# Batch 0's first tiles as seven block products, last value groups in 64 rows, and a new order up to pair 17

## The chip, the cores and the metric

The kernel runs on one core of one Trainium2 chip. The metric is the device time of one execution in microseconds. The five engines are named as the profile does: PE (matmuls; PEld is its weight loads), DVE, ACT, POOL and SP, which issues most DMAs.

## What is computed

Cosine attention over 8 batches of 12 heads, 448 positions and 64 columns a head, followed by a two-layer network with a hard-swish between:

```python
q_n = q / (np.linalg.norm(q, axis=-1, keepdims=True) + 1e-06)
k_n = k / (np.linalg.norm(k, axis=-1, keepdims=True) + 1e-06)
scores = np.matmul(q_n, k_n.transpose(0, 1, 3, 2)) / tau
attn = softmax(scores)
x = np.matmul(attn, v)                  # to (3584, 768)
h = x @ w_in                            # (768, 2048)
g = h * np.clip(h + 3.0, 0.0, 6.0) / 6.0
out = g @ w_out                         # (2048, 768)
```

## The kernel before

Heads are taken two at a time: 6 pairs a batch, 48 pairs in all. For each pair, the steps have two-letter names, which the written order uses. `LQ` and `LV` load q, k and v (DMAs on SP). `SQ` squares an item, on ACT, POOL or DVE as its letter says; `RE` sums the squares (DVE, L236); `NO` makes the reciprocal norms with four activations (ACT, L252 to L255); `NM` multiplies them in (mostly POOL, L267). An item j is one pair's-worth of q or k; its raw data lie in a ring of buffers in the large tile `big`. `TR` transposes on PE (up to item 13), `XD` by a transposing DMA on SP from item 14 on; `CQ`, `CK` and `CS` copy the result to where scores read it. `SC.i.g` are the scores of pair i, in four groups g: three of 2 x 128 keys and a last one, M, that holds the last 64 keys of both heads; they are matmuls over 64 rows (L415). `EX` takes their exponentials (ACT, L433). `VC` casts the values, `VA.i.g` multiplies exponentials by values into the PSUM tile PV (L455, 8 matmuls of 65 columns a group), and `FI` divides by the row sums (DVE, L475 and L476). `BK` with `CX`, or the DMAs `XP` and `XB`, bring the result into `xT`.

The network's work is a stream of units taken from by `U`. A first-layer unit (`mm1_unit`, L566) is 6 matmuls of 448 columns; `UA` is its clip on ACT (L575) and `UV` the product on DVE (L581), which writes `gT`. The second layer runs on output tiles of 128 tokens. Before the change, batch 0's tiles 0 to 2 are six units `mm2_unit` (3 tiles, two halves of the output columns, 16 matmuls of 384 columns each, L613). All other tiles are taken in pairs, as a 2 x 2 block product with seven products instead of eight: `product_unit` (L739, 8 matmuls each), named 1 to 7, with sums of g (`g_sum`, L717, DVE), sums of w_out's blocks (`weight_sums`, L688, DVE) and sums of results on POOL (`both`, `rest`, L768 to L772, and L780). The sums y3 and y4 are written over blocks of w_out, so they come after the last unit that reads those blocks, and after sums 1 and 6, or 1 and 7, which read them too.

Six PSUM banks serve as a ring for scores, transposes and units; a bank is taken again once its readers are done. Each engine runs its instructions in the order in which they are written. Up to pair 17 that order is `PLAN`, a list of steps written out by hand, with `ORDER` saying which units the stream holds; from pair 18 (`FIRST`) on it is a loop with fixed places, its units in `units` and its sums in `side`. In the plan the last value group reads all 128 rows, the other head's half of the value tile being zero; in the loop it reads 64:

```python
rows = slice(64 * h, 64 * h + 64) if name == "M" and i >= FIRST else slice(0, 128)
```

`D` and `DP` are matmuls on zeros that fill PE early on. `W` starts one of eight DMAs of weights on POOL's queue.

Of the kernel before, what the change touches and what calls it, by code (L numbers as in the profile page):

```python
# [10 lines left out]
AF = mybir.ActivationFunctionType  # L11
# [3 lines left out]
EPS = 1e-6  # L15


FIRST = 18
ORDER = "111111111111111111111111111111222222"

PLAN = [
# [36 lines left out]
]  # L58


# [1 line left out]
def kernel(  # L62
# [10 lines left out]
    nc = tc.nc  # L73
    B, H, S, D = q.shape
# [59 lines left out]

    def raw_before(j):

        return j - NR if j < 26 else j - NR + 2

    def raw_buffer(j):
        return raws[j % NR if j < 26 else (j - 26) % (NR - 2)]  # L140

    sqs = [item(NR + i) for i in range(2)]
    nrms = [const.tile([128, 7, 2, D], BF16, name=f"nrm{i}", tag=f"nrm{i}") for i in range(3)]
# [21 lines left out]
    def needs(*what):  # L165
        for w in what:
            assert w in issued or any(x < 0 for x in w[1:] if isinstance(x, int)), w
# [76 lines left out]
    def norms(d, *items):  # L244

        needs(("NM", 2 * d - 4), ("NM", 2 * d - 3))
        items = items or (0, 1)
        for x in items:
            needs(("RE", 2 * d + x))
        it = slice(items[0], items[-1] + 1)  # L250
        ln, nr, le, r = (t[:, it, :] for t in rs[d % 2])
        nc.scalar.activation(out=ln, in_=n2s[d % 2][:, it, :], func=AF.Ln)  # L252
        nc.scalar.activation(out=nr, in_=ln, func=AF.Exp, scale=0.5)
        nc.scalar.activation(out=le, in_=nr, func=AF.Ln, bias=EPS)
        nc.scalar.activation(out=r, in_=le, func=AF.Exp, scale=-1.0)  # L255
        for x in items:
            issued.add(("NO", d, x))

# [184 lines left out]
    def q_cols(b, j):  # L443
        return slice(128 * j, 128 * j + 128)

    def values(i, g):
        needs(("VC", i), ("FI", i - 1), *values_after(i, g))
        at = at_of.pop((i, g))
        vt = vx[i % NVX]
        last = g == (3 if i < FIRST else 2)  # L450
        for n, name in enumerate(GROUPS[g]):
            for j in range(4):
                for h in (range(2) if name == "M" else ["AB".index(name[0])]):
                    rows = slice(64 * h, 64 * h + 64) if name == "M" and i >= FIRST else slice(0, 128)
                    nc.tensor.matmul(  # L455
                        pv_out(j, h),
                        at[rows, n, q_cols(i // HP, j)],
                        vt[rows, 3 + h if name == "M" else 5 * h + int(name[1]), :],
                        start=(name in ("A0", "B0") and j == 0),
                        stop=last,  # L460
                        skip_group_check=True,
                    )
# [67 lines left out]
    def tail(c, n):  # L530

        assert 2 * RAW <= c and c + n <= (NR + 2) * RAW + NV * VAL
        return big[:, c : c + n]
# [102 lines left out]

    def second(b):
        assert b % 2 == 0
        return [(mm2_unit, b, t, m) for m in (1, 0) for t in range(3)]

# [1 line left out]


    LEFT, RIGHT = slice(0, MH), slice(MH, 2 * MH)
    PAIRS = [p for b in range(0, B, 2) for p in (((b, 0), (b, 1)), ((b + 1, 3), (b + 1, 0)), ((b + 1, 1), (b + 1, 2)))][1:]
    LOOP = 8
    summed, g_summed, issued_products = set(), set(), set()
    banks, parts, ready = {}, {}, set()  # L650
    late_sums = [
# [3 lines left out]
    late_sums[0].pop("e")  # L655
    TAIL += 7 * SUM
    wide = [big[:, c : c + MH] for c in range(0, 3 * MH, MH)]
    wide_late = [tail(c, MH) for c in range(TAIL, TAIL + 2 * (len(PAIRS) - LOOP) * MH, MH)]

    def sum_of(n, what):  # L660

        if what == "e":
            return gs["1"] if n < B - 2 else late_sums[1]["e"]
        if n < LOOP or n == len(PAIRS) - 1:
            return gs[what + str(n % 2) if what == "7" else what]
        return late_sums[n % 2][what]

# [2 lines left out]
            return wide[n % 2], wide[2]  # L670
        return wide_late[2 * (n - LOOP) : 2 * (n - LOOP) + 2]

    def weight_sums(what, c0, n):

        w = w_out_sb[:, :, :].rearrange("p (c k) m -> p c k m", k=2)[:, c0 : c0 + n]
        b11, b12, b21, b22 = (w[:, :, k, m] for k in range(2) for m in (LEFT, RIGHT))
# [8 lines left out]
        }[what]  # L685
        if what in w_sum:
            o = w_sum[what][:, c0 : c0 + n, :]
        nc.vector.tensor_tensor(out=o, in0=x, in1=y, op=op)  # L688
        summed.update((what, c) for c in range(c0, c0 + n))

    def half(b, t, k):
# [143 lines left out]
    def sums(n, names):  # L835
        return [(g_sum, n, x) for x in names]
# [4 lines left out]
    def products(text):  # L841
# [17 lines left out]
    }  # L859
    APART = {(n, y) for n in range(len(PAIRS)) for x, y in (("5a", "3"), ("2a", "4")) if f"{x}.{n}" in " ".join(TURNS.values()).split()}  # L860
    side = {
        18: [(weight_sums, "y4", KC // 2, KC // 2)], 19: sums(0, "62"), 20: sums(0, "1"),
        21: sums(1, "75"), 22: sums(1, "621"),
        25: sums(2, "75"), 26: sums(2, "62"), 27: sums(2, "1"), 28: [(g_left, 2)], 29: sums(2, "e"),
        31: sums(3, "75"), 32: sums(3, "62"), 33: sums(3, "1"),
# [70 lines left out]
    def finish_units(e):  # L936
        post[e].pop(0)()

    def whole_units(n, engines="av"):
# [4 lines left out]
                    finish_units(e)  # L944

    OPS = {
        "LQ": load_qk, "LV": load_v, "W": next_weights, "SQ": square, "RE": reduce, "NO": norms,
        "NM": normalise, "VC": vcast, "TR": transposes, "XD": crossbar, "XB": back_crossbar, "XP": back_two, "CQ": copy_q, "CK": copy_k, "CS": copy_k3, "SC": scores,
        "EX": exps, "VA": values, "FI": finish_values, "BK": back, "CX": copy_x, "U": unit, "UA": lambda: finish_units("a"), "UV": lambda: finish_units("v"),
        "GL": g_left, "WS": lambda x, *h: weight_sums(str(x), *((h[0] * KC // 2, KC // 2) if h else (0, KC))), "UU": whole_units, "D": busy, "DP": busy_pv, "OPEN": open_ring,  # L950
    }

    def do(op, *args):
        OPS[op](*args)
        key = (op,) + tuple(a for a in args if isinstance(a, int))
        if op not in ("RE", "NM", "LQ"):
            issued.add(key[:3] if op == "SC" else key)

    def run(text):
# [133 lines left out]
```

## Time and profile before

| | us |
|---|---|
| median of 3 runs (405.72 to 407.1) | 405.85 |
| the profiled execution's own time | 405.02 |
| its span, first to last instruction | 403.2 |
| PE busy | 394.5 |
| DVE busy | 286.4 |
| ACT busy | 266.2 |
| POOL busy | 233.2 |
| granted PE clock, mean | 1.00 of full |

The span starts with the first instruction and ends with the last; busy time is a union, and matmuls overlap, so that a busy PE can still hold gaps between starts. Stretches of the span are told in us from its start. The unchanged first steps of the plan end near 34 us, pair 18 begins near 113 us.

### The profile page before, as it was taken

The numbers are of one execution on the slowest core, as the hardware profiler recorded it, in microseconds if no ns is written. First come the engines' busy times: TensorE is split into PE (matmuls) and PEld (weight loads), VectorE is DVE, ScalarE is ACT, GpSimd is POOL, SyncE is SP. The second block draws the span as 40 slices with busy tenths as digits, with TensorE's granted clock in tenths as the row PEclk, the third lists the DMA queues.
The fourth block names the chain that finished last, engine by engine and source line by source line (L and its number), as shares of the span: only waits on it lengthen the run. The fifth ranks groups of instructions, "written<-read, shape, count | busy, mean of one in ns | idle before, by whom it ended". The sixth has DMA issues, their size and how long they took to land.

```text
span 403.2 us, 9617 instructions
## 1 busy us (share of the span) xinstructions
PE 394.5 (98%) x3696; PEld 233.7 (58%) x3696; DVE 286.4 (71%) x501; ACT 266.2 (66%) x609; POOL 233.2 (58%) x228
## 2 busy tenths in 40 slices
PE   7999999999989999999999999999999999999996
PEld 5666556555655556555555556555565556555564
DVE  6898768766998676776857878687656666644663
ACT  6899998787557686776758768668648755224230
POOL 7899664562294996489386875776665500510070
PEclk9999999999999999999999999999999999999999
DMA  8999989989989559885989659986864523130133
GB/s 290 308 241 276 200 249 239 144 126 221 193 204 231 120 119 228 176 224 130 181 214 210 134 143 171 183 193 145 191 150 82 112 46 67 40 79 20 27 73 99
DMA packets 91566, 65.32 MB, mean 162 GB/s; under 512 B 56064, under 2 KB 89984, under 8 KB 91520
## 3 DMA queue, kind: packets, MB, share of 16 engines
q1 hardware_dynamic: 87408, 58.02, 62.8%
q0 software_dynamic: 3712, 6.29, 9.1%
q8 instruction: 29, 0.48, 0.5%
q10 hardware_dynamic: 400, 0.39, 0.3%
q14 instruction: 17, 0.14, 0.1%
HBM read 47.19 MB, written 11.01 MB: 144 GB/s over the span
## 4 chain that ended last, share of the span: by engine, by line
PE 94%; DVE 3%; DMA 1%; POOL 1%; ACT 0%; issue 0%; SPq 0%; DVEq 0%
PE M L566 24%; PE M L739 17%; PE PV L455 13%; PE Y L566 6%; PE M L415 6%; PE Z L566 5%; PE Y L739 4%; PE Z L739 4%; PE M L613 3%; PE M L819 2%; PE Z L415 2%; PE PV L921 2%; PE Z L819 1%; PE Y L415 1%; PE SC L415 1%; DMA big<-in_q_dram 1%
## 5 line engine op out<-in xcount | busy, mean ns | idle before, releaser
L433 ACT ACTIVATE at<-M 128x448 bf16<-128x448 f32 x200 | 99.6, 565 | 17.7 <-PE M L415 15.5
L566 PE MATMUL M<-xT,w_in_sb 128*128 128x448 bf16 x522 | 110.7, 353 | 0.0
L566 PEld LDWEIGHTS <-w_in_sb 128*128 128x128 bf16 x768 | 71.9, 98 | 62.5 <-issue 2.6
L267 POOL TENSOR_TENSOR nrm<-big,r 128x896 bf16<-128x896 f32 (+1 forms) x48 | 79.4, 1658 | 26.7 <-ACT r L255 18.5
L581 DVE SCALAR_TENSOR_TENSOR gT<-u,M 128x448 bf16<-128x448 bf16 x76 | 46.8, 618 | 35.6 <-ACT u L575 35.3
L455 PEld LDWEIGHTS <-at 128*128 128x128 bf16 (+1 forms) x1536 | 54.8, 97 | 24.1 <-issue 14.8
L224 POOL TENSOR_TENSOR big<-big 128x896 f32<-128x896 f32 (+3 forms) x39 | 63.8, 1639 | 8.0 <-DMA big<-in_k_dram 4.1
L575 ACT ACTIVATE u<-M 128x448 bf16<-128x448 f32 x87 | 48.8, 561 | 29.5 <-PE M L566 29.1
L455 PE MATMUL PV<-vx,at 128*128 128x65 bf16 (+1 forms) x1536 | 64.3, 194 | 0.2 <-DVE on L476 0.2
L236 DVE TENSOR_REDUCE n<-big 128x14 f32<-128x896 f32 (+1 forms) x50 | 51.8, 1040 | 3.9 <-ACT big L222 3.4
L372 POOL COPY km<-tT 64x128 bf16<-64x128 bf16 x34 | 12.4, 364 | 59.3 <-DMA tT<-nrm 43.4
L768 POOL TENSOR_TENSOR big<-big 128x384 f32<-128x384 f32 x11 | 12.0, 1088 | 55.1 <-ACT big L787 55.0
L739 PEld LDWEIGHTS <-gT 128*128 128x128 bf16 x288 | 27.8, 98 | 20.2 <-DVE gT L717 0.6
L739 PE MATMUL M<-w_out_sb,gT 128*128 128x384 bf16 x208 | 37.9, 326 | 0.1
L433 ACT ACTIVATE at<-Z 128x448 bf16<-128x448 f32 x49 | 27.6, 564 | 10.4 <-PE M L415 8.8
L286 POOL CAST vx<-big 128x512 bf16<-128x512 f32 x44 | 33.0, 754 | 2.4 <-DMA big<-in_v_dram 2.4
L476 DVE TENSOR_TENSOR on<-PV,rc 128x512 bf16<-128x512 f32 x48 | 33.2, 691 | 1.7
L415 PE MATMUL M<-tT,kz 64*128 64x448 bf16 (+1 forms) x175 | 31.9, 351 | 1.0 <-DVE o L626 1.0
L739 PEld LDWEIGHTS <-gs 128*128 128x128 bf16 x224 | 21.6, 98 | 14.5
L566 PE MATMUL Y<-xT,w_in_sb 128*128 128x448 bf16 x132 | 28.6, 353 | 0.0
L433 ACT ACTIVATE at<-Y 128x448 bf16<-128x448 f32 x45 | 25.6, 568 | 3.3 <-PE Z L415 3.1
L739 PE MATMUL M<-w_sum,gs 128*128 128x384 bf16 x144 | 26.3, 326 | 0.0
(131 smaller groups left out, 553.9 us busy)
## 6 DMA issues: line engine op xcount, KB each, us to landing
big<-in_v_dram SPq DMA_DIRECT2D x96, 128.0 KB, 4.7
big<-in_k_dram SPq DMA_DIRECT2D x24, 448.0 KB, 4.9
big<-in_q_dram SPq DMA_DIRECT2D x24, 448.0 KB, 4.3
out_dram<-o SPq DMA_DIRECT2D x107, 96.0 KB, 2.2
w_in_sb<-in_moe_w_in_dram POOLq DMA_DIRECT2D x4, 768.0 KB, 9.1
w_out_sb<-in_moe_w_out_dram POOLq DMA_DIRECT2D x4, 768.0 KB, 9.7
tT<-nrm SPq DMA_TRANSPOSE x34, 3.4
xT<-on SPq DMA_TRANSPOSE x25, 3.8
```

Of the source, the lines that this page charges most:

```text
L224: engines[e].tensor_tensor(out=o, in0=i, in1=i, op=ALU.mult)
L236: nc.vector.tensor_reduce(out=n2s[d % 2][:, j % 2, c], in_=sq[:, :, :, :].rearrange("p g c d -> p (g c) d")[:, c, :], axis=AX.X, op=ALU.add,)
L267: engines[e].tensor_tensor(out=nrm[:, :, g, :].rearrange("p c g d -> p g c d"), in0=raw_of[j][:, g, :, :], in1=rs[d % 2][3][:, j % 2, :] . ...
L286: (engines[e].copy if e == "a" else engines[e].tensor_copy)(out=o, in_=f)
L415: nc.tensor.matmul(o, ks, qt[rows], start=True, stop=True)
L433: nc.scalar.activation(out=o, in_=x, func=AF.Exp, scale=inv_tau)
L455: nc.tensor.matmul(pv_out(j, h), at[rows, n, q_cols(i // HP, j)], vt[rows, 3 + h if name == "M" else 5 * h + int(name[1]), :], start=(name ...
L476: nc.vector.tensor_tensor(out=on[:, :, :, :].rearrange("p j h d -> p h j d"), in0=pv4[:, :, :, 0:D], in1=rc[:, :, :].to_broadcast([128, 2, ...
L566: nc.tensor.matmul(ps[:, 0:S], w_in_sb[:, cc, fc * 128 : (fc + 1) * 128], x[:, cc, 0:S], start=(cc == 0), stop=(cc == CC - 1),)
L575: nc.scalar.activation(out=u[:, :], in_=ps[:, 0:S], func=AF.Relu, bias=0.5, scale=1.0 / 6.0)
L581: nc.vector.scalar_tensor_tensor(out=g[:, fc, c0 : c0 + S], in0=u[:, :], scalar=1.0, in1=ps[:, 0:S], op0=ALU.min, op1=ALU.mult,)
L739: nc.tensor.matmul(m, lhs[:, c, :], rhs[:, c, c0 : c0 + width], start=(base is None and c == 0), stop=(c == KC - 1), skip_group_check=True,)
```

## The change

The steps of the plan up to the opening of the ring of PSUM banks (`OPEN`) stay. From there to pair 17's turn the order is a new one, with these differences in what is done:

- Batch 0's tiles 0 and 1 become a block product of number -1 (`FOREMOST`): seven products of 8 matmuls in place of four units of 16. Tile 2 keeps its two units of 16. The products' sums of g (`GS.-1.x`, five) and their result sums on POOL (`UP`, the operations of `both`, `rest` and two additions) are new; the products 5 and 2 stand apart from 3 and 4, in banks of their own.
- The sums of w_out are made in halves and earlier: eight halves on DVE, two (of sums 6 and 7) on POOL. The half of y4 that ran beside pair 18 goes into the plan.
- The last value groups of pairs 4 and 6 to 16 read 64 rows (`.h`).
- Norms 6 run as two activations (`NA`) and two DVE operations (`ND`).
- Three filler matmuls go. Some squares, casts and copies change engine: ACT takes three value casts and seven more copies, DVE four more casts.
- The raw items 19 to 25 use five buffers instead of seven (as items from 26 on did before), since the two others hold the new product's results.

```diff
-ORDER = "111111111111111111111111111111222222"
+ORDER = "111111111111111111111111111111222222222"
...
-    "BK.3.Y VA.4.1 LQ.12 CS.6.v OPEN DP.2 CX.3.v NO.5 SC.6.0 VA.4.2 VA.4.3 SC.6.1 SC.6.2 EX.6.0 NM.8.p FI.4 EX.6.1",
+    "BK.3.Y VA.4.1 LQ.12 CS.6.v OPEN NO.5 NM.8.p CX.3.a SC.6.0 VA.4.2 VA.4.3.h SC.6.1 SC.6.2 NM.9.p EX.6.0 FI.4",
...
-    "CK.17.v XD.18 U EX.16.1 SQ.20.a.0.7 NM.19.p FI.15 WS.6 U UV XD.19 SC.16.3 RE.20 GL.0 WS.1 WS.7.0 EX.16.2 U VA.16.0 UA VA.16.1 LV.11",
...
-    "XP.14 NO.10 FI.16 NM.20.p CK.18.v U CK.19.v WS.7.1 WS.y3 WS.y4.0 XB.16 EX.17.2 UV UA VA.17.0 VC.18.p EX.17.3 RE.22 CS.18.v",
...
+    "LQ.19 VA.12.3.h UA U RE.17 NO.8 GS.-1.6 GL.0 GS.-1.7 UA UV U FI.12 EX.13.2 NM.17.p U UV VC.15.v CK.14.v U",
+    "VA.13.0 UA UV SC.13.3 NM.16.p XD.17 U W U UA UA SQ.19.a.0.7 SQ.18.p.0.7 U CS.14.v WS.1.v.0 UV UV LV.9 RE.19",
+    "UA UA SC.14.0 WS.6.p.0 CK.15.v EX.13.3 U UV UA LV.8 VA.13.1 EX.14.0 RE.18 UA U VA.13.2 UV UA UV VC.14.a",
+    "VA.13.3.h SC.14.1 EX.14.1 UV SQ.20.a.0.7 UV SC.14.2 FI.13 U EX.14.2 LQ.22 UA U SC.14.3 WS.1.v.1 EX.14.3",
+    "WS.7.p.0 WS.6.v.1 GS.-1.2 UA NO.9 U WS.y3.v.0 WS.y3.v.1 LQ.21 WS.7.v.1 U UV VA.14.0 XD.16 UV WS.y4.v.0",
+    "SC.15.0 UA WS.y4.v.1 SC.15.1 EX.15.0 GS.-1.5 SC.15.2 VA.14.1 VC.17.a VA.14.2 NM.18.v U EX.15.1 SC.15.3 U",
...
-        return j - NR if j < 26 else j - NR + 2
+        return j - NR if j < 19 else j - NR + 2
...
+    def powers(d, *items):
...
+        nc.scalar.activation(out=ln, in_=n2s[d % 2][:, it, :], func=AF.Ln)
+        nc.scalar.activation(out=nr, in_=ln, func=AF.Exp, scale=0.5)
...
+    def reciprocals(d, *items):
...
+        nc.vector.tensor_scalar_add(out=le, in0=nr, scalar1=EPS)
+        nc.vector.reciprocal(out=r, in_=le)
...
-                    rows = slice(64 * h, 64 * h + 64) if name == "M" and i >= FIRST else slice(0, 128)
+                    apart = name == "M" and (i >= FIRST or halves)
+                    rows = slice(64 * h, 64 * h + 64) if apart else slice(0, 128)
...
-        return [(mm2_unit, b, t, m) for m in (1, 0) for t in range(3)]
+        return [(mm2_unit, b, 2, m) for m in (1, 0)] + products(f"3.{FOREMOST} 4.{FOREMOST} 5a.{FOREMOST} 2a.{FOREMOST} 1.{FOREMOST} 6.{FOREMOST} 7.{FOREMOST}")
...
-    def weight_sums(what, c0, n):
+    def weight_sums(what, c0, n, e="v"):
...
-        nc.vector.tensor_tensor(out=o, in0=x, in1=y, op=op)
+        engines[e].tensor_tensor(out=o, in0=x, in1=y, op=op)
...
-        18: [(weight_sums, "y4", KC // 2, KC // 2)], 19: sums(0, "62"), 20: sums(0, "1"),
+        19: sums(0, "62"), 20: sums(0, "1"),
```

More of the change, by code (lines that the diff above doesn't have):

```diff
@@ L135, in raw_before @@
     def raw_before(j):
-        return j - NR if j < 26 else j - NR + 2
+        return j - NR if j < 19 else j - NR + 2
     def raw_buffer(j):
-        return raws[j % NR if j < 26 else (j - 26) % (NR - 2)]
+        return raws[j % NR if j < 19 else (j - 19) % (NR - 2)]
     sqs = [item(NR + i) for i in range(2)]
@@ L255, in norms @@
         nc.scalar.activation(out=r, in_=le, func=AF.Exp, scale=-1.0)
+        for x in items:
+            issued.add(("NO", d, x))
+    def powers(d, *items):
+        needs(("NM", 2 * d - 4), ("NM", 2 * d - 3))
+        items = items or (0, 1)
+        for x in items:
+            needs(("RE", 2 * d + x))
+        it = slice(items[0], items[-1] + 1)
+        ln, nr = (t[:, it, :] for t in rs[d % 2][:2])
+        nc.scalar.activation(out=ln, in_=n2s[d % 2][:, it, :], func=AF.Ln)
+        nc.scalar.activation(out=nr, in_=ln, func=AF.Exp, scale=0.5)
+        for x in items:
+            issued.add(("NA", d, x))
+    def reciprocals(d, *items):
+        items = items or (0, 1)
+        for x in items:
+            needs(("NA", d, x))
+        it = slice(items[0], items[-1] + 1)
+        nr, le, r = (t[:, it, :] for t in rs[d % 2][1:])
+        nc.vector.tensor_scalar_add(out=le, in0=nr, scalar1=EPS)
+        nc.vector.reciprocal(out=r, in_=le)
         for x in items:
@@ L444, in q_cols, with values @@
         return slice(128 * j, 128 * j + 128)
-    def values(i, g):
+    def values(i, g, halves=""):
         needs(("VC", i), ("FI", i - 1), *values_after(i, g))
@@ L638, in second @@
         assert b % 2 == 0
-        return [(mm2_unit, b, t, m) for m in (1, 0) for t in range(3)]
+        return [(mm2_unit, b, 2, m) for m in (1, 0)] + products(f"3.{FOREMOST} 4.{FOREMOST} 5a.{FOREMOST} 2a.{FOREMOST} 1.{FOREMOST} 6.{FOREMOST} 7.{FOREMOST}")
     LEFT, RIGHT = slice(0, MH), slice(MH, 2 * MH)
-    PAIRS = [p for b in range(0, B, 2) for p in (((b, 0), (b, 1)), ((b + 1, 3), (b + 1, 0)), ((b + 1, 1), (b + 1, 2)))][1:]
-    LOOP = 8
+    PAIRS = [p for b in range(0, B, 2) for p in (((b, 0), (b, 1)), ((b + 1, 3), (b + 1, 0)), ((b + 1, 1), (b + 1, 2)))]
+    FOREMOST, LAST, LOOP = -1, len(PAIRS) - 2, 8
+    PAIRS = dict(enumerate(PAIRS, FOREMOST))
     summed, g_summed, issued_products = set(), set(), set()
@@ L657 @@
     wide = [big[:, c : c + MH] for c in range(0, 3 * MH, MH)]
-    wide_late = [tail(c, MH) for c in range(TAIL, TAIL + 2 * (len(PAIRS) - LOOP) * MH, MH)]
+    wide_late = [tail(c, MH) for c in range(TAIL, TAIL + 2 * (LAST + 1 - LOOP) * MH, MH)]
     def sum_of(n, what):
@@ L663, in sum_of @@
             return gs["1"] if n < B - 2 else late_sums[1]["e"]
-        if n < LOOP or n == len(PAIRS) - 1:
+        if n < LOOP or n == LAST:
             return gs[what + str(n % 2) if what == "7" else what]
@@ L859 @@
     }
-    APART = {(n, y) for n in range(len(PAIRS)) for x, y in (("5a", "3"), ("2a", "4")) if f"{x}.{n}" in " ".join(TURNS.values()).split()}
+    APART = {(n, y) for n in PAIRS for x, y in (("5a", "3"), ("2a", "4")) if n == FOREMOST or f"{x}.{n}" in " ".join(TURNS.values()).split()}
     side = {
-        18: [(weight_sums, "y4", KC // 2, KC // 2)], 19: sums(0, "62"), 20: sums(0, "1"),
+        19: sums(0, "62"), 20: sums(0, "1"),
         21: sums(1, "75"), 22: sums(1, "621"),
@@ L946 @@
     OPS = {
-        "LQ": load_qk, "LV": load_v, "W": next_weights, "SQ": square, "RE": reduce, "NO": norms,
+        "LQ": load_qk, "LV": load_v, "W": next_weights, "SQ": square, "RE": reduce, "NO": norms, "NA": powers, "ND": reciprocals,
         "NM": normalise, "VC": vcast, "TR": transposes, "XD": crossbar, "XB": back_crossbar, "XP": back_two, "CQ": copy_q, "CK": copy_k, "CS": copy_k3, "SC": scores,
-        "EX": exps, "VA": values, "FI": finish_values, "BK": back, "CX": copy_x, "U": unit, "UA": lambda: finish_units("a"), "UV": lambda: finish_units("v"),
-        "GL": g_left, "WS": lambda x, *h: weight_sums(str(x), *((h[0] * KC // 2, KC // 2) if h else (0, KC))), "UU": whole_units, "D": busy, "DP": busy_pv, "OPEN": open_ring,
+        "EX": exps, "VA": values, "FI": finish_values, "BK": back, "CX": copy_x, "U": unit, "UA": lambda: finish_units("a"), "UV": lambda: finish_units("v"), "UP": lambda: finish_units("p"),
+        "GL": g_left, "GS": lambda n, what: g_sum(n, str(what)), "WS": lambda x, e, *h: weight_sums(str(x), *((h[0] * KC // 2, KC // 2) if h else (0, KC)), e), "UU": whole_units, "D": busy, "DP": busy_pv, "OPEN": open_ring,
     }
@@ L955, in do @@
         key = (op,) + tuple(a for a in args if isinstance(a, int))
-        if op not in ("RE", "NM", "LQ"):
+        if op not in ("RE", "NM", "LQ", "NA", "ND"):
             issued.add(key[:3] if op == "SC" else key)
```

39 rows, old and new, of the table PLAN are left out of this document.

## The prediction

> **What bounds the kernel now.** I read the page's engine totals first, then busy time by stretch, then the chain that ended last, then the groups and the timeline for prices.
>
> ```profile
> span 403.2 us, 9617 instructions
> PE 394.5 (98%) x3696; PEld 233.7 (58%) x3696; DVE 286.4 (71%) x501; ACT 266.2 (66%) x609; POOL 233.2 (58%) x228
> ```
> ```profile
> 34.40:67.00 32.60, 32.60 (x411) 20.22 (x409) 24.29 (x59) 29.95 (x72) 19.14 (x19) 1.00 1.02 235
> 67.00:90.00 23.00, 23.00 (x219) 12.36 (x217) 16.90 (x31) 18.40 (x43) 16.40 (x16) 1.00 0.92 152
> 90.00:112.60 22.60, 22.60 (x205) 13.56 (x204) 18.85 (x27) 15.26 (x37) 7.08 (x7) 1.00 1.03 207
> 112.60:120.00 7.40, 6.39 (x64) 3.60 (x63) 7.08 (x7) 3.74 (x9) 7.26 (x7) 1.00 0.87 217
> ```
>
> The rows of the second view are stretches: their length, then busy time of PE, weight loads, DVE, ACT, POOL, then clock, DMA share, GB/s. PE is full from the changed part's first microsecond (about 34) to pair 18, at full clock. Only the last stretch shows a hole, and there DVE is full instead. So the change pays one for one where it takes work from PE, and loses one for one wherever another engine comes late. ACT has 2.7 us of slack in the first 33 us; DVE has about 6 us in the next 23.
>
> The hole, in the chain and in the timeline:
>
> ```profile
> 111.86 2.62 PE M L613 x16
> 114.47 0.03 DVEq L626
> 114.51 1.36 DVE w_out_sb L688
> 115.87 0.48 DVE o L626
> ```
> ```profile
> 111.34 4.52 DVE L688 TENSOR_TENSOR w_out_sb<-w_out_sb 128x3072 bf16<-128x3072 bf16 x2
> 115.79 0.54 DVE L626 COPY o<-M 128x384 f32<-128x384 f32 x1
> ...
> 111.00 1.97 POOL L267 TENSOR_TENSOR nrm<-big,r 128x896 bf16<-128x896 f32 x1 [7.67 <-ACT r L255]
> 112.92 2.14 POOL L286 CAST vx<-big 128x512 bf16<-128x512 f32 x1
> ```
>
> A PSUM bank waits for the copy of L626, and the copy waits behind two weight sums. The same place shows a price that matters below: the whole sum took 3.24 us (group L688) where the undisturbed one at 104.57 took 1.75. It started at 111.34, with POOL's L267 running to 112.97, and 112.97 + 1.65 is its end; POOL's cast, alone about 0.6 us, was stretched to 2.14. The two take turns.
>
> Prices on PE, from the timeline (starts are what counts, since matmuls overlap):
>
> ```profile
> 68.93 0.41 PE L455 MATMUL PV<-vx,at 128*128 128x65 bf16 x8
> 69.28 0.36 PE L415 MATMUL Z<-tT,kz 64*128 64x448 bf16 x1
> ...
> 130.81 0.29 PE L455 MATMUL PV<-vx,at 64*128 64x65 bf16 x8
> 130.95 0.54 PE L415 MATMUL M<-tT,kz 64*128 64x448 bf16 x3
> ```
>
> Eight values of 128 rows run 0.35 us up to scores in 64 rows: 8 x 0.029 plus about 0.10 for the step from 128 to 64 rows. Eight of 64 rows run 0.14, two at a time.
>
> **The change part by part, against the profiled execution's own 405.0 us (span 403.2, 1.8 around it). The median of the runs is 405.85; differences are carried over to it.**
>
> PE work. Six block products of 16 matmuls become two of 16 and seven of 8: 96 - 88 = 8 matmuls of 128x384 less. Eight such take 1.30 us in the chain: -1.3. Three filler matmuls go, about 0.1 each: -0.3. Twelve last groups in 64 rows: 0.23 - 0.14 = 0.09 each, -1.1. By the order of instructions, PE steps between 128 and 64 rows 77 times each way instead of 76: one pair more, +0.2. Sum -2.5.
>
> By the Trainium skill (TensorEngine Tiling (Array Packing), Key Properties) a change of tiling mode drains the array, which speaks against halves among full-height matmuls. The trace agrees, at about 0.1 us a step.
>
> The old hole. The y3 and y4 sums move ahead of pair 15's scores, and the half sum beside pair 18 goes: -1.4.
>
> ACT in pairs 6 to 9. It takes a copy of x (0.51), two small key copies (no row on ACT; DVE's are 0.19) and a value cast (0.5, from its 448 columns at 0.54), and gives up a square (0.94) only behind them. ACT hid these under PE, with 2.7 us of slack over 33. When they are no longer hidden, exponentials free PSUM banks later and the scores wait. Bounds 0 and 1.0 us; I take +0.3.
>
> The seven products' operands. The first product (name 3) needs the y3 sum, which needs both halves of sums 1 and 6 and the end of the block product that reads the right half of w_out. From the scores of pair 13 to that product PE has 11 first-layer units (12.5), two block products (5.2), two pairs' scores and six value groups with their steps (3.4): 21.1 us. DVE has in the same stretch, each at its mean less the 0.08 by which neighbours overlap: 13 gate products of L581 (7.0), 4 reductions (4.0), 2 value normalisations (1.7), 3 sums of g (1.8), the left copy (0.4), a cast (0.6), two key copies (0.5), 5 half weight sums at 0.87 (4.35), a piece of a square (0.15): 20.5. Up to the second product DVE adds 3.6 (three halves, one gate product, one store), PE 2.7. So 24.1 against 23.8: no slack before any turn-taking, where the old stretch 67 to 112.6 had 35.8 of 45.6. Turn-taking in before: seven weight sums took 13.0 us for 9.05 undisturbed, 4.0 lost, 0.57 an operation. In after POOL is idle at the three sums of g and after its own two half sums, so I count two collisions (one with POOL's half sum, one with pair 19's normalisation) at about 1 us, against 0.6 us of lead: +0.9. Bounds 0 (DVE always first) and 11 x 0.57 = 6.3, for its eight half sums and three sums of g.
>
> POOL's two half sums (128x1536) have no row. POOL takes 1.0 us for 384 and 1.68 for 896 columns: from 2.6 (slope 1.33 ns) to 4.0 (four times 1.0); I take 3, nearer the longer row. By the Trainium skill (GPSIMD Engine Reference, Elementwise) two-input work runs at 2.6 cycles an element: an estimate of 3.3 us, within that range.
>
> What else moves without a price. Loads of q and k 19 to 25 have five buffers instead of seven, so each waits for the normalisation five places earlier; all of these end before the load's turn on SP, the last by some 3 us. The transpose for pair 18's queries stands on SP behind two result stores that wait for POOL's additions: copy 0.8, addition 1.0, stores 1.2, issue and landing 3.5 to 6.6, against 7.5 us of PE work; it is covered at the usual landing and costs up to 2 at the longest. Norms 6 are split between ACT and DVE, 1.6 us ahead of need. POOL's squares, moved back from ACT, are needed by reductions later. PE covers all of these; the loop from pair 18 on is unchanged.
>
> Sum: -2.5 - 1.4 + 0.3 + 0.9 = -2.7. That is 402.3 on the profiled execution, 403.2 on the median.
>
> **The rivals.** (a) Everything is covered and no new wait appears: -2.5 - 1.4 = -3.9, 402.0. For it: outside the hole PE lost almost nothing under the old order. Against: DVE's 24.1 against 23.8. (b) The turn-taking eats the gain: a wait of 3 to 4 us in place of 0.9, about 405.8. (c) The halves save nothing, since half of them would pay their steps: -2.7 + 1.1 = -1.6, 404.3; the order's 77 steps speak against it. (d) Slower: DVE and POOL take turns all through pairs 13 and 14, at 0.57 us for each of the 11 operations, 6.3 in all in front of the second product: -2.5 - 1.4 + 0.3 + 6.3 = +2.7, 408.6. It makes the kernel slower from 3.6 us on, by over 0.5% from 5.6. For it: the 3.24 and 2.13 us sums, and two more POOL operations as long as 3 us in just that stretch. Against: POOL has about 15 us of work in these 26.
>
> By the Trainium skill (SBUF — State Buffer, Who interferes with whom) a DVE instruction with two SBUF inputs and a GpSimd instruction that reads SBUF exclude each other for the whole instruction, whichever came second; this rule is (d). The trace agrees at 111.34, and shows too that an operation begun first runs undisturbed (g sum at 133.16: 0.68 with POOL starting inside it).
>
> **How the numbers follow.** 0.5% of 405.85 is 2.0 us, about what a measurement of this kernel can tell from no change. Forecast 0.36 and (a) 0.24 are faster: 0.60. (b) 0.12 and (c) 0.04 are within: 0.16. (d) 0.24 is slower. The predicted time is the forecast's, 403.2. The range goes from 401.5, under (a), to 409.0, which takes in (b), (c) and more than half of (d), the rest of which, with waits at further places, is left out with less than 2 in 10.
>
> **What would show it.** PE with 3685 matmuls and about 2.5 us less of them; no wait of L415 on DVE's L626 at pair 18; weight sums on DVE between 0.9 and 2 us, two on POOL of about 3; a hole on PE under 1.5 us ahead of the first seven-product matmuls. A hole of over 4 us there, with DVE's sums stretched beside POOL's, is (d). A hole at pairs 6 to 9 with ACT full, or scores of pair 18 waiting for a transpose, would put the loss where I have counted almost none.

## The result, and the profile after

The changed kernel takes 404.22 us (median of 9 runs, 403.21 to 405.28) against 405.63 for the kernel before on the same chip (9 runs, 405.19 to 407.12): ratio 0.9958, 95% interval 0.9943 to 0.9974. That is a gain of 1.4 us where 2.65 was forecast. On another chip (run E0 below) the ratio was 0.9996 (0.9979 to 1.0014), so that the size of the gain, 1.4 us on one chip and 0.2 on the other, is not settled by the medians. The profiled spans on both chips are the same, 402.3 against 403.2 before, so 0.9 us is what the traces have to explain.

The page's first lines and busy time by stretch, of the changed kernel:

```profile
span 402.3 us, 9629 instructions
PE 392.8 (98%) x3685; PEld 232.2 (58%) x3685; DVE 287.8 (72%) x509; ACT 269.3 (67%) x620; POOL 236.6 (59%) x230
```
```profile
34.40:67.00 32.60, 32.45 (x404) 19.18 (x402) 25.22 (x57) 29.27 (x75) 20.12 (x18) 1.00 0.98 222
67.00:90.00 23.00, 22.96 (x201) 12.69 (x199) 20.94 (x36) 18.03 (x41) 16.27 (x17) 1.00 0.94 188
90.00:112.60 22.60, 22.60 (x240) 13.53 (x237) 19.19 (x30) 19.41 (x45) 10.46 (x11) 1.00 0.94 211
112.60:120.00 7.40, 5.83 (x62) 3.40 (x59) 4.84 (x9) 4.59 (x11) 6.08 (x5) 1.00 0.78 175
```

PE (second number of each row) holds 0.15 us of waiting in the first stretch where it held none, and in the last stretch 1.57 us where it held 1.01. DVE, full in that last row before (7.08 of 7.40), has 2.6 us to spare: what PE waits for there is no longer DVE. The chain that ended last names it:

```profile
109.89 0.35 PE Z L769 x2
110.24 4.10 DMA tT<-nrm
...
114.39 0.36 PE Y L443
```

For 4.1 us the chain runs through one DMA, the transpose XD.19 for pair 18's queries, and PE's scores (L443) start as it lands. Further on the chain leaves PE at 118.5 and comes back to it at 136.3 only, again by way of SP:

```profile
122.13 0.66 SPq L536
...
122.89 3.54 DMA tT<-nrm
...
131.15 2.36 POOL o L810 x2
...
135.69 0.57 DVE big L826
136.30 1.46 PE M L769 x8
```

To see the whole, I took the starts of the last 3361 matmuls of before, and of the same 3350 of the changed kernel (both from 33.7 us on). A start that comes over 0.1 us later than the matmul ahead of it takes (0.189 for 448 columns, 0.162 for 384, 0.029 for 65) is a wait; steps from 64 to 128 rows, 0.09 to 0.12 each, count as work, unless a wait falls on one: that wait is then counted whole, the step in it. A wait is placed at the start of the matmul ahead of it.

| | from the first of these to the end, us | of it waits | the rest, work |
|---|---|---|---|
| before | 365.57 | 1.64 | 363.93 |
| changed | 364.60 | 3.63 | 360.97 |
| difference | -0.97 | +1.99 | -2.96 |

The work fell by more than forecast. The waits of before (1.17 at pair 18, 0.17 at 120.8, 0.30 at 225.0) are all gone, and new ones of 3.63 us took their place: 0.28, 0.14, 0.20 and 0.20 at 35.5, 37.7, 40.9 and 68.8; 1.74 at 112.6 for XD.19; 0.58 at 124.7, where a first-layer unit waits for pair 17's transpose (XB.17); and 0.50 at 135.6, where the first loop product waits for the chain shown above.

SP's timeline shows why XD.19 was late. Before the change:

```profile
101.07 1.80 SPq L323 DMA_TRANSPOSE tT<-nrm  x1
...
104.56 1.82 SPq L323 DMA_TRANSPOSE tT<-nrm  x1
```

And in the changed kernel (start, length, SP's queue, line, what is issued):

```profile
104.56 1.24 SPq L351 DMA_TRANSPOSE tT<-nrm  x1
105.89 1.18 SPq L630 DMA_DIRECT2D out_dram<-o  x2
107.13 1.79 SPq L198 DMA_DIRECT2D big<-in_q_dram  x1
109.02 1.12 SPq L630 DMA_DIRECT2D out_dram<-o  x2
110.24 1.28 SPq L351 DMA_TRANSPOSE tT<-nrm  x1
```

Most issues hold SP for about 0.6 us, a transpose for 1.25, and the next one starts at once; a few take longer, as the load of 1.79 above and both transposes of before. From 99 to 127 us SP is busy 26.0 of 28 us with 31 issues; it was before, too (25.3, also 31). What changed is the order on that full queue: XD.18 moved from 101.07 to 104.56 and XD.19 from 104.56 to 110.24.

### The profile page after: what moved, and what is told of

It reads as the page before. It is cut to its first block, busy times and chain, and to the rows that moved or that the text cites. A ratio compares the mean times of both kernels' runs of the same rounds, so it can differ in the third digit from the quotient of the medians.

```text
span 402.3 us, 9629 instructions
## 1 busy us (share of the span) xinstructions
PE 392.8 (98%) x3685; PEld 232.2 (58%) x3685; DVE 287.8 (72%) x509; ACT 269.3 (67%) x620; POOL 236.6 (59%) x230
## 4 chain that ended last, share of the span: by engine, by line
PE 91%; DVE 2%; DMA 2%; POOL 2%; ACT 1%; issue 1%; SPq 0%; POOLq 0%; ACTq 0%
PE M L595 22%; PE M L769 16%; PE PV L484 11%; PE Y L595 7%; PE Z L595 6%; PE M L443 6%; PE Z L769 6%; PE Y L769 4%; PE M L849 3%; PE PV L951 3%; DMA tT<-nrm 2%; PE Y L443 1%; PE Z L443 1%; ACT at L461 1%; PE SC L443 1%
## 5 line engine op out<-in xcount | busy, mean ns | idle before, releaser
L595 PE MATMUL M<-xT,w_in_sb 128*128 128x448 bf16 x492 | 104.4, 353 | 0.0
L295 POOL TENSOR_TENSOR nrm<-big,r 128x896 bf16<-128x896 f32 (+1 forms) x47 | 78.0, 1664 | 23.5 <-ACT at L461 9.5
L604 ACT ACTIVATE u<-M 128x448 bf16<-128x448 f32 x82 | 46.2, 563 | 30.6 <-PE M L595 29.7
L610 DVE SCALAR_TENSOR_TENSOR gT<-u,M 128x448 bf16<-128x448 bf16 x71 | 43.3, 618 | 27.7 <-ACT u L604 27.5
L769 PEld LDWEIGHTS <-gT 128*128 128x128 bf16 x320 | 30.9, 98 | 21.8 <-issue 0.4
L769 PE MATMUL M<-w_out_sb,gT 128*128 128x384 bf16 x216 | 39.4, 326 | 0.0
L505 DVE TENSOR_TENSOR on<-PV,rc 128x512 bf16<-128x512 f32 x48 | 33.2, 691 | 1.7
L769 PEld LDWEIGHTS <-gs 128*128 128x128 bf16 x248 | 23.8, 98 | 16.8 <-issue 1.0
L443 PE MATMUL M<-tT,kz 64*128 64x448 bf16 (+1 forms) x177 | 31.9, 351 | 0.0
L461 ACT ACTIVATE at<-Y 128x448 bf16<-128x448 f32 x47 | 27.0, 575 | 6.8 <-PE Z L443 6.7
L595 PE MATMUL Z<-xT,w_in_sb 128*128 128x448 bf16 x138 | 30.0, 353 | 0.4 <-DMA xT<-on 0.4
L769 PE MATMUL M<-w_sum,gs 128*128 128x384 bf16 (+1 forms) x152 | 26.4, 318 | 0.3 <-DVE big L826 0.3
```

Source lines behind the costliest of these rows:

```text
L295: engines[e].tensor_tensor(out=nrm[:, :, g, :].rearrange("p c g d -> p g c d"), in0=raw_of[j][:, g, :, :], in1=rs[d % 2][3][:, j % 2, :] . ...
L443: nc.tensor.matmul(o, ks, qt[rows], start=True, stop=True)
L461: nc.scalar.activation(out=o, in_=x, func=AF.Exp, scale=inv_tau)
L505: nc.vector.tensor_tensor(out=on[:, :, :, :].rearrange("p j h d -> p h j d"), in0=pv4[:, :, :, 0:D], in1=rc[:, :, :].to_broadcast([128, 2, ...
L595: nc.tensor.matmul(ps[:, 0:S], w_in_sb[:, cc, fc * 128 : (fc + 1) * 128], x[:, cc, 0:S], start=(cc == 0), stop=(cc == CC - 1),)
L604: nc.scalar.activation(out=u[:, :], in_=ps[:, 0:S], func=AF.Relu, bias=0.5, scale=1.0 / 6.0)
```

## The experiments

The theory after this reading (queue): what PE saved was waited for at three places that the order on SP's queue sets. Its rivals: DVE's turn-taking with POOL ate the gain; or SP is simply full, so that order does not matter.

### E1: XD.19 directly behind XD.18

```diff
-    ... CK.17.v XD.18"
+    ... CK.17.v XD.18 XD.19"
-    ... VA.16.0 XD.19 EX.17.0 ...
+    ... VA.16.0 EX.17.0 ...
```

> The changed kernel with the transpose for pair 18's queries issued on SP directly behind pair 18's keys' transpose (about 105.9), ahead of the four result stores and a load that it stood behind. Theory (queue): the 1.64 us wait of PE at 112.6 is that transpose's landing at 114.34; issued at about 105.9 it lands at about 109.5 and the wait goes, 1.0 to 1.6 us below the changed kernel, about 402.6 to 403.2. Rival 1 (turn-taking of DVE with POOL took the missing gain): the wait stays or is replaced at once by one on DVE, time as the changed kernel's, 404.2. Rival 2 (SP is full from 99 to 130 us, so any order costs the same): the four stores and the later transposes come 1.3 us later, the waits at 124.7 and 135.6 grow by what is gained at 112.6, time as the changed kernel's within 0.4 us.

Measured: 405.68 us, ratio to before 1.0015 (0.9988 to 1.0042). The changed kernel did not run on this chip; on the two where it did, its ratio was 0.9958 and 0.9996. The wait at 112.6 is gone, and nothing is gained. The timeline of PE in E1, in brackets the idle time ahead of a row and what ended it:

```profile
123.37 1.11 PE L595 MATMUL Z<-xT,w_in_sb 128*128 128x448 bf16 x5
126.61 0.35 PE L595 MATMUL Z<-xT,w_in_sb 128*128 128x448 bf16 x1 [2.13 <-DMA xT<-on]
```

The wait for XB.17 grew from 0.58 to 2.30 (start to start), and one of 0.61 appeared at 109.9. XB.17's data were ready at 116.8 (the division of L505), but it was issued at 122.32, since four value loads (LV.11), XB.16, four stores and a load stood ahead. So rival 2's consequence came true. Whether its reason did, that any order costs the same, is for E5 and E6.

### E2: the same transpose late, in the kernel before

```diff
-    ... U UV XD.19 SC.16.3 ...
+    ... U UV SC.16.3 ...
-    ... EX.17.1 LV.10 U SC.17.3"
+    ... EX.17.1 LV.10 XD.19 U SC.17.3"
```

> The kernel before with that same transpose moved the other way on SP: behind a load of q and k and four value loads, so issued at about 113.7 instead of 104.56. Theory (queue): it lands 3.6 us after its issue, at about 117.3 to 118.6, against pair 18's first scores at about 116.3 after the old wait of 1.36 us: PE waits 1.0 to 2.3 us more, time 406.6 to 408. Rival 1 (turn-taking alone sets these places): no change, 405.6 within 0.5. Rival 2 (full SP queue): no change as well, but with the waits further on smaller by as much.

Measured: 407.15, ratio 1.0057 (1.0030 to 1.0084), inside what the queue theory expected. The chain of E2 at that place (this execution, at 411.75 us, was the slowest of the 12; its first 34 us took 36.9, so all its times are 3.2 later):

```profile
117.26 3.54 DMA tT<-nrm
...
120.93 0.36 PE M L415 x2
```

One moved transpose makes this wait in the kernel before too. DVE's and POOL's sums are untouched there.

### E3: the changed kernel without the halves

The edit takes `.h` off the twelve last value groups.

> The changed kernel with its twelve last value groups in 128 rows again, all else kept. If the halves pay on the path what they pay on PE: 12 x 0.09 = 1.1 us slower, about 405.3. If what is saved ahead of pair 18 is only waited for there (the transpose lands when SP's queue gets to it): ten or eleven of the twelve lie ahead of that wait, so the wait at 112.6 shrinks from 1.64 to about 0.7 and the time rises by 0.1 to 0.4 only, about 404.5. If the halves pay nothing on PE: 404.2.

Measured: 405.98, ratio 1.0006 (0.9984 to 1.0027). By the count above: work 362.65 (+1.68 against the changed kernel), waits 2.61 (-1.02). The three waits at 112 to 136 shrank from 2.82 to 2.03. So the halves are worth more on PE than I counted, and 0.8 of those 1.7 us were being waited for at pair 18 and behind it. The order without them steps between 128 and 64 rows 79 times each way instead of 77, and one step pair costs 0.19 here (medians of the starts in this trace: 0.098 down, 0.093 back): (1.68 - 2 x 0.19) / 12 = 0.11 us for one group, or 0.12 if the two steps that fall on waits in this execution are counted as work.

### E4: the halves alone, in the kernel before

The edit gives `values` its `halves` argument, as in the change, and puts `.h` on the same twelve groups.

> The kernel before with the same twelve last value groups in 64 rows, in its own order, where about seven of them stand next to scores of 64 rows and five (pairs 10, 12, 13, 15, 16) between steps of 128 rows. If a step from 128 to 64 rows and back costs about 0.2 us: 7 x -0.09 + 5 x (0.2 - 0.09) = -0.1 us, time as before's 405.6. If the step costs nothing: -1.1 us, 404.5. In the trace: PE's starts around an isolated group show the step directly.

Measured: 405.25, ratio 0.9994 (0.9974 to 1.0014): no gain. Work 363.70, -0.23, with 82 step pairs instead of 76. (0.23 + 6 x 0.19) / 12 = 0.11, about the price of a group in E3. Both runs are explained by 0.11 to 0.12 for a group and 0.19 for a pair of steps; halves between steps of full height give back more than they save.

### E0: the changed kernel again, beside E5 to E7

> The changed kernel unchanged, on the chip and in the rounds of the next three, as what they are compared with. Both theories: 404 to 405, with waits of PE of about 1.7 us at 112.6, 0.6 at 124.7 and 0.5 at 135.6.

Measured: 405.13; before on this chip 405.29. Waits of 1.28, 0.59 and 0.48 at the three places, work 360.95 as in the first trace.

### E5: LV.11 behind the transposes

```diff
-    ... EX.17.1 XP.14 LV.11 U U XB.16 ...
+    ... EX.17.1 XP.14 U U XB.16 ...
...
             prepare(("XD", i + 2))
+        if i == FIRST:
+            do("LV", 11)
```

> The changed kernel with the four value loads of LV.11 (4 x 0.67 us on SP, ahead of pair 16's transpose) issued behind pair 17's and pair 20's transposes instead; pair 18's query transpose stays late. Theory (one SP queue, each wait set by what stands ahead on it): the wait at 112.6 stays 1.7, pair 17's transpose is issued 2.7 us earlier (about 118.9, landing about 122.8), so the wait at 124.7 (0.58) goes, and the one at 135.6 (0.50), which hangs on pair 20's transpose, shrinks or goes: 0.6 to 1.1 us below the changed kernel. Rival (SP is only full because the loads and stores behind it are slow, and what is moved out comes back as longer issues): no change.

Measured: 404.04, 1.1 below E0 (ratio to before 0.9967, 0.9946 to 0.9988). The waits at 124.7 and 135.6 are gone. In the profiled execution, though, 0.56 was added at pair 18 and 0.76 at 111, where XD.18 landed late (4.45 us after its issue instead of 2.75), so that the trace alone shows a gain of 0.1 against E0. The median carries the verdict, and only just.

### E6: both moves

> Both moves: pair 18's query transpose directly behind its keys', and LV.11 behind the transposes of pairs 17 and 20. Theory (one SP queue): all three waits go, 1.7 + 0.6 + 0.5 = 2.8, less the 0.6 that appeared at 109.9 when the first move was made alone; 2.0 to 2.8 us below the changed kernel, about 401.6 to 402.4. If the two moves are worth no more together than the second alone (the queue's total work between 99 and 126 us is the limit, not its order): about 0.6 to 1.1 below the changed kernel.

Measured: 402.33, 2.8 below E0, ratio to before 0.9927 (0.9900 to 0.9953). Busy time by stretch of E6, the last two rows:

```profile
90.00:112.60 22.60, 21.80 (x224) 12.90 (x222) 18.87 (x30) 19.45 (x46) 10.19 (x11) 1.00 0.98 201
112.60:120.00 7.40, 7.40 (x72) 4.37 (x70) 5.54 (x11) 4.68 (x11) 6.08 (x5) 1.00 0.85 180
```

PE is full from 112.6 on: the three waits (2.34 us in E0) are gone, and one of 0.97 at 109, in the row above, has come, with the same DMAs on the same engines. The order was the limit, not SP's total. By the count of starts E6 is 1.6 below E0, by the medians 2.8; E1 alone is 0.6 above the changed kernel by that count, E5 alone 0.1 below E0 (1.1 by the medians). The two together are worth more than their sum, since each alone hands its wait to the place that the other mends.

### E7: and pair 3's copy of x on DVE again

The edit is `CX.3.a` to `CX.3.v`.

> Both moves, and pair 3's copy of x back on DVE, as in the kernel before. If the waits of 0.28, 0.14, 0.20 and 0.20 us at 35.5, 37.7, 40.9 and 68.8 come from that one copy in front of ACT's work: the first three go, 0.5 to 0.6 us below the kernel with both moves. If they come from ACT's load in pairs 6 to 9 as a whole: the first goes and the others stay, 0.1 to 0.3 below. If DVE is late there instead: no change, or up to 0.3 above.

Measured: 401.97, ratio 0.9908 (0.9884 to 0.9931), 0.4 below E6 with overlapping intervals. In the trace the wait at 35.5 falls from 0.28 to 0.11 and that at 37.7 goes; so 0.3 of the early waits was ACT's one copy. The wait at 40.9 is another matter. There a first-layer unit starts at 41.11, right behind the landing of a quarter of w_in at 40.98, and it was 0.20, 0.36, 0 and 0 in the changed kernel, E0, E6 and E7: a load's landing, not ACT. The one at 68.8 stays in every run: scores wait for a PSUM bank that DVE's product of L610 frees at 68.98.

What E7 has left is that wait at 109, 1.03 here. Its chain:

```profile
104.72 4.48 DMA tT<-nrm
...
109.23 0.04 DVE kz L390
...
109.50 0.56 DVE big L826
...
110.10 1.46 PE Z L769 x8
```

DVE's key copy waits for XD.18's landing and stands in front of the addition that frees the next product's bank.

### E8: two moves more

```diff
-    ... GS.-1.2 UA NO.9 ... VA.14.0 XD.16 UV ...
+    ... GS.-1.2 XD.16 UA NO.9 ... VA.14.0 UV ...
-    ... VA.16.1 CK.18.v UV"
+    ... VA.16.1 UV CK.18.v"
```

> The version with both moves and pair 3's copy on DVE, and two moves more against the 1.03 us wait that it has left at 109: the transpose XD.16, whose landing (102.05) lets POOL's normalisation 19 start after 10.1 us of waiting, goes ahead of two result stores and a load on SP (issued about 94 instead of 98), and on DVE the addition that frees the first product's bank goes ahead of the key copy that waits for XD.18's landing (109.20). Theory (the wait at 109 is POOL's chain and that landing, both set by SP's order): the wait shrinks to 0.3 or less, about 0.7 to 1.0 us below the version without the two moves, 401.0 to 401.3. Rival (DVE or ACT, not SP, is what is late there): no change.

Measured: 401.42, ratio 0.9882 (0.9856 to 0.9908). The wait at 109 is gone, by the second move: XD.18 landed at 110.37, and the addition had run ahead of the key copy, at 109.68. The first move brought little: XD.16 was issued 1.9 us earlier than in E7 but landed at 101.86, hardly earlier (102.05), so POOL started no sooner. Other waits came at 97 to 104, where DVE's sums were late: the last quarter of w_out landed at 93.40 in this execution, at 91.22 in the changed kernel's. Start for start they cost 1.0 us against E7, as much as was gained at 109, so the profiled execution is no shorter than E7's (362.34 against 362.29 by the count of starts). The medians, 0.55 apart, come from two chips, and their intervals overlap: that E8 is faster than E7 is not shown.

### E9: E8 without the halves

> The same with the twelve last value groups in 128 rows again. In the changed kernel their removal lengthened the profiled run by 0.7 only, since 0.8 us of it came out of the waits at 112 to 136. If those waits are what took the gain, here, without them, the halves are worth what they are on PE: 12 x 0.09 = 1.1 to 1.5 us slower than the version with halves. If something else takes it: 0.4 to 0.8.

Measured: 404.08, ratio 0.9949 (0.9924 to 0.9975), 2.7 above E8 and more than either theory gave. By the count of starts E9 is 2.24 longer (364.59 against 362.34), and 0.66 of that is a wait at 40.9 for w_in. The other 1.6 is about the worth of the halves on PE (1.7 by E3, with the steps they spare). So where nothing downstream waits for SP they show nearly all of it; in E3, 0.8 came out of the waits at 112 to 136. The rest of the 2.7 lies within the spread of these runs (402.46 to 406.51).

### E10: E8 with POOL's two half sums on DVE

The edit is `WS.6.p.0` and `WS.7.p.0` to `.v.0`.

> The same as the first of these with POOL's two half weight sums on DVE: 2 x 0.95 us more on DVE ahead of the y3 sum, less the 0.6 that one of DVE's sums lost by waiting for POOL. In the changed kernel the y3 sum ended 0.6 us before the first of the seven products was reached, and the y4 sum just when the second was. If that is all the lead there is: a new wait of PE of 0.7 to 1.3 us at the first two products, and the time longer by as much. If POOL's sums cost DVE more by turn-taking than they save: no change or faster.

Measured: 401.55, ratio 0.9893 (0.9861 to 0.9926): no difference from E8, and PE's waits are down to 0.44. The lead of 0.6 us was not all the lead there was. DVE's timeline in E8, and in E10:

```profile
93.50 1.83 DVE L718 TENSOR_TENSOR w_sum<-w_out_sb 128x1536 bf16<-128x1536 bf16 x2 [1.80 <-DMA w_out_sb<-in_moe_w_out_dram]
```
```profile
91.52 2.69 DVE L718 TENSOR_TENSOR w_sum<-w_out_sb 128x1536 bf16<-128x1536 bf16 x3
```

In E8 DVE stands idle for 1.8 us until w_out has landed. In E10 the load landed at 90.38. Of the two extra halves, one (at 85.89) uses up 0.76 us that DVE stood idle at 89.9 in the changed kernel. The other is the third sum of the row above: three take 2.69 where the changed kernel's two take 2.39, because these two lost 0.58 beside POOL's half sum (rows further below). So the second of the two expected outcomes came, and POOL's turn-taking is one part of the reason, the idle time the other. The y3 sum ends at 96.55, 0.26 ahead of the first product (96.81); in the changed kernel it was 0.59 (96.75, 97.34). E8 and E10 are the fastest versions here, 1.1 to 1.2% below the kernel before; by the count of starts E10 is 2.8 below E0 (361.42 to 364.26) at the same work (360.97 to 360.95): all of it is waits.

## Why the prediction was right or wrong

**PE work: right in kind, 0.46 more than counted.** -2.96 against -2.5. The halves were undersized, about 0.11 each instead of 0.09 (E3 and E4 agree), which is 0.24 of it; the step pair is 0.19 as taken. The remaining 0.2 is not assigned.

**The old hole: right.** Gone, with two smaller waits that I had not counted; -1.64 against -1.4.

**ACT in pairs 6 to 9: right in place, +0.3 forecast.** Of 0.82 measured, 0.4 stands where forecast and 0.3 of it is one copy (E7). 0.2 is the landing of w_in and 0.2 a bank that DVE frees. ACT's busy time in that stretch fell, from 29.95 to 29.27, so it was the place of one copy and not ACT's load. (Seven copies move to ACT in the new order, but three that it made before go back to DVE.)

**The seven products' operands: wrong, +0.9 forecast, none measured.** The y3 sum ended at 96.75, 0.6 ahead of the product. The counts up to the first product were good: PE took 21.2 us from the scores of pair 13 (76.17) to it, for 21.1 counted, and DVE's operations took 20.85, for 20.5. What the count left out is that the two do not start together. DVE began the first of the counted operations, two gate products, at 74.56, 1.6 us before PE reached those scores. It then lost 0.76 to idle time and 0.58 to one collision, and 0.6 of lead was left: 21.17 + 1.61 - 20.85 - 0.76 - 0.58. Of the collisions, one took place, and it cost what one was priced at: two DVE halves took 2.39 instead of 1.81, while POOL's half sum ran to 92.73.

```profile
92.02 2.39 DVE L718 TENSOR_TENSOR w_sum<-w_out_sb 128x1536 bf16<-128x1536 bf16 x2
94.94 1.81 DVE L718 TENSOR_TENSOR w_out_sb<-w_out_sb 128x1536 bf16<-128x1536 bf16 x2
```

POOL's half sums took 3.09 (3 taken; the estimate from the Trainium skill (GPSIMD Engine Reference, Elementwise) was 3.3). Rivals (b) and (d), which hung on this turn-taking, fall with it. In E10 normalisation 19, 1.69 in the changed kernel, took 4.16 beside DVE's sums, which kept their 1.82: the Trainium skill's rule of (d) (SBUF — State Buffer, Who interferes with whom) did act, but mostly on POOL. Rival (c) gave 404.3, nearly the time measured, for a reason that does not hold: the halves do pay on PE (E3, E9).

**What moved without a price: here the prediction failed.** The transpose for pair 18's queries "is covered at the usual landing and costs up to 2 at the longest", so it went into the sum at nothing, though scores of pair 18 waiting for a transpose were named as a sign of being wrong. XD.19 cost 1.74, and XB.17 and XD.20, which the text did not look at, 1.08 more. The step took the wait for POOL's additions as what delays the queue. The second addition ended at 107.0, and its stores were issued at 109.02, because SP was still issuing (its rows are above; POOL's row of that addition here).

```profile
106.01 0.99 POOL L810 TENSOR_TENSOR o<-o,big 128x384 f32<-128x384 f32 x1 [0.43 <-ACT o L806]
```

I had priced one dependency and not summed the queue: 26 us of issues in 28, with the transposes now behind stores and loads that nobody waits for. Two moves on that queue took these waits away (E6), and one on DVE the wait that then came to light (E8, E10).

The sum in the profiled execution: 0.5 more off PE's work, 0.2 more off old waits and no collision (0.9) make 1.6 better than forecast; a queue that was not counted (2.8) and 0.5 more waiting in pairs 6 to 11 make 3.3 worse. That is -1.0 where -2.7 was forecast (in the medians -1.4 and -2.65). The total came nearer than its parts, because the two errors pull against each other; that much of it is luck.

## What to carry to other kernels

When a new order is written, sum the issues of each DMA queue between the old place and the new one as one sums an engine's work, and put the transfers that an engine waits for ahead of loads and stores with slack; on a full queue a single move only hands the wait to the next transfer (E1), and the price of an order shows when all of them are in place (E6). Work taken from the busiest engine pays only as far as the next fixed landing (E3). A count of work against work says nothing of lateness without the points at which the two engines start: here DVE had a lead of 1.6 us over PE in the changed kernel, and in E8 a weight load's landing held it back.

## What the runs showed of the hardware that was not expected

In the profiled execution of E2, PE soon ran at half its clock after the 3.1 us wait (to 120.93). Busy time by stretch of E2, columns as above; the third last is the granted clock:

```profile
120.90:122.30 1.40, 1.37 (x29) 0.95 (x30) 0.00 (x0) 0.98 (x3) 1.40 (x2) 1.00 0.61 135
122.30:125.60 3.30, 3.30 (x17) 1.43 (x13) 1.94 (x4) 2.49 (x6) 1.21 (x2) 0.50 0.69 137
```

Half speed for 3.3 us costs 1.65 more, half again the wait itself; after the 1.74 us wait of the changed kernel and the 2.30 of E1 the clock stayed at 1.00. By the Trainium skill (TensorE: Matmul & The Clock Gate, Why this matters for your kernels) idle gaps of more than about 3 us drop the clock to half. The trace agrees at this place, but the same execution was at half clock from 13.09 to 16.51 as well, after an idle gap of only 1.93 us.

The 13 traces show a pattern. In E2 the clock changed at 13.09, 16.51, 122.32 and 125.73, all of them whole multiples of 3.413 us from the first record of the clock, at 6.27; so do the changes in the other 12 traces (one in each, after the last matmul). Cut each trace into slots of that length: wherever PE was idle for 1.93 us or more of a slot (1.93 and 2.03 in E2), the next one was at half clock, and nowhere after 1.92 or less. A grid line cut E1's idle gap of 2.13 into 0.54 and 1.59. So a wait's length alone does not tell; that is a reading of the traces, in which the ends of matmuls are modelled, not something that was tried.

The landing of a transpose varied far more than its issue: XD.18 landed 2.7 us after its issue in the changed kernel, E0, E1, E3, E9 and E10, and 4.5 to 5.2 after it in E5 to E8. The traffic of E7 between 107 and 110 us (40 slices of 75 ns) shows the DMA engines moving at most 14 GB/s for 14 slices, 1.05 us, with that transpose not landed:

```profile
GB/s 0 0 0 34 154 242 266 280 263 239 72 14 0 0 10 4 7 10 10 10 10 10 7 10 14 184 280 290 280 290 367 266 61 123 143 61 287 144 308 246
```

E0 has such a stretch at 108.8 (at most 41 GB/s), when XD.18 had landed. What makes these stretches was not tried, nor whether they are what delays the transpose; but with landings of 2.7 to 5.2 us, 3 us of cover is not safe here.
